# Token-mixing MLP products in pairs of tiles by Strassen's scheme: seven products of quarters in place of eight

## The chip, the cores and the metric

The kernel runs as one program on one core of one Trainium2 chip. The metric is the time of one execution on the device in microseconds (us). The kernel before takes 1084.5 us (the median of 3 runs, 1084.46 to 1085.56).

## The reference

A network of four layers on x of 2048 tokens (S) by 640 channels (D): a spectral filter A and a token-mixing MLP B, and the same two again with the same weights, each with a residual and a layer norm in front.

```python
def _A_ref(x, w_r, w_i):
    X = jnp.fft.rfft2(x, axes=(-2, -1)) * (w_r + 1j * w_i)
    return jnp.fft.irfft2(X, s=(S, D), axes=(-2, -1))

def _B_ref(x, w1, b1, w2, b2):          # F = 1728
    h = _layernorm(x, axis=-1)
    u = _gelu(jnp.einsum("bsd,sf->bdf", h, w1) + b1)
    y = jnp.einsum("bdf,fs->bds", u, w2) + b2
    return y.transpose(0, 2, 1)

x = A_x
x = x + _A_ref(_layernorm(x, axis=-1), A_w_r, A_w_i)
x = x + _B_ref(_layernorm(x, axis=-1), B_w1, B_b1, B_w2, B_b2)
x = x + _A_ref(_layernorm(x, axis=-1), A_w_r, A_w_i)
x = x + _B_ref(_layernorm(x, axis=-1), B_w1, B_b1, B_w2, B_b2)
```

## The kernel before, in words

The change is in the two MLP layers (`b(li)`: `first` is the first MLP layer, `last` the last layer of the network) and in the edges of the spectral parts `a1` and `a2` that prepare them. The float32 products of the MLP are made of three float16 ones: each operand is split into a high half (the value scaled by a power of two and rounded to float16) and a low half (what is left), and TensorE adds high·high, high·low and low·high in PSUM. For weights, ACT writes the high half `wh` from the float32 load `raw`, and DVE the low half `wl` = raw·s − wh; for the normed hidden state `hf` the halves are `hh` and `hl`, for the gelu's output `uh` and `ul`.

The first product of a layer has 14 tiles of 128 columns of F (`ft`); the last holds its 64 columns twice, which lets one of its three products be left out. Each tile sums over 16 row tiles `j` of the tokens, in two column halves of 320 (one PSUM bank each): 96 matmuls. The second product has 16 tiles of tokens that each sum over the 14 tiles of F. Tiles 0 and 1 of a layer begin with the products that need only `hh`, so that DVE has time for `hl`. After a tile ACT and DVE make the gelu: ACT `t` (affine) and `q` (square) from PSUM, a DVE step, ACT's tanh, a DVE step, then the split into `uh` and `ul`.

Weights are loaded as halves of 512 KB by SP's queue, three tiles ahead (`wload`), and split one tile ahead (`prep`, `wsplit`). In the first MLP layer the scale of each weight tile has to be found first: ACT squares the loads with a sum (`scan1`, tile `junk`), TensorE adds over the partitions, small steps on DVE and POOL make a power of two (`scale1`); the last layer uses the scales again. `scale_u` gives the scale of the gelu's output.

What runs on each engine is in program order, and in the MLP the order is that of the code (`self.pin = True` writes the instructions as they come; otherwise a planner may place them). Nearly all instructions go through one helper, line 46 (L46) of the profile of before, so groups are told apart by the names of tiles: `raw` weights as loaded, `ps` PSUM, `xt` the residual rows.

Of the kernel before, what the change touches and what calls it, by code (L numbers as in the profile page):

```python
# [18 lines left out]
NJ, NG, NFT = 16, 16, 14  # L19
EPS = 1e-5  # L20
# [3 lines left out]
HA = range(8)  # L24
# [4 lines left out]
US = 2.0 ** 14  # L29
# [3 lines left out]
EXPO = 0x7F800000  # L33

# [19 lines left out]
class Layers:  # L54
# [41 lines left out]
    def setup(self):  # L96
# [16 lines left out]
        self.qt = base.tile([128, NFT], F32, name="qt")  # L113
        self.su, self.iu = (base.tile([128, 1], F32, name=a) for a in ("su", "iu"))
# [41 lines left out]
    def total(self, sq):  # L156
# [6 lines left out]
        ps = self.big()[:, 0, :n]  # L163
        self.PE.matmul(ps, self.ones, b, start=True, stop=True)
        yield ps
# [17 lines left out]
    def scan1(self, m, cs=(0, 1)):  # L183
        if m < NFT + NJ:
            if 0 in cs:
                self.ssq = self.t(self.base, [128, 1, 2], F32, "sq", 2)
            for c in cs:
                self.scan(self.wraws[m][c], self.ssq[:, 0, c:c + 1])

    def scale1(self, m):  # L190

        V, (k, t, _) = self.V, self.wtile(m)
        c = slice(t, t + 1)
        q = self.t(self.base, [128, 1], F32, "q2", 2) if k else self.qt[:, c]
        for ps in self.total(self.ssq):
            yield
        V.tensor_scalar(q, ps, SMALL, WS ** -2, op0=ALU.max, op1=ALU.mult)
        i = self.pow2(q, self.st[k][:, c])
        V.tensor_scalar(self.ct[k][:, c], i, self.iu if k else 0.5 / ZS, None, op0=ALU.mult)
        yield  # L200
# [39 lines left out]
    def scale_u(self):  # L240

        V, b = self.V, self.base
        q, qc = (b.tile([128, 1], F32, name=a) for a in ("qm", "qc"))
        V.tensor_reduce(q, self.qt, op=ALU.max, axis=mybir.AxisListType.X)
        V.scalar_tensor_tensor(qc, q, 2.0 * S * D * (WS / US) ** 2, self.qb, op0=ALU.mult, op1=ALU.add)
        i = self.pow2(qc, self.su)
        V.tensor_scalar(self.iu, i, 0.125, None, op0=ALU.mult)
# [153 lines left out]
    def a1(self, first):  # L401
# [3 lines left out]
        ph = self.push("ha", side=self.sq)  # L405
        self.hh = {j: ph.tile([128, 2, 320], F16, name=f"hh{j}_{self.n}") for j in HA}
# [159 lines left out]
        quarter = lambda q: ((q // 2,), slice(q % 2 * 4, q % 2 * 4 + 4))  # L566
# [11 lines left out]
        for g in range(NG - 1):  # L578
# [18 lines left out]
            if 10 <= g < 14:  # L597
                self.wsplit(0, quarter(g - 10)[0], hi=False, part=quarter(g - 10)[1])
# [12 lines left out]
            if g == 3:  # L611
                self.wload(0)
                self.wopen(0)
# [4 lines left out]
            if first and g in (5, 6):  # L618
                self.scan1(0, (g - 5,))
            if first and g == 7:  # L620
                sc0 = self.scale1(0)
            if first and 7 <= g < 10:
                next(sc0)
            if 9 <= g < 13:
                self.wsplit(0, quarter(g - 9)[0], lo=False, part=quarter(g - 9)[1])
# [37 lines left out]
        self.pin = False  # L663
        self.pop("a1")
# [3 lines left out]
    def a2(self, li):  # L668
# [4 lines left out]
        self.wp[1] = self.push("wb", side=self.sp)  # L673
        ph = self.push("hf", side=self.sp)
        self.hf = [ph.tile([128, 2, 320], F32, name=f"hf{j}_{self.n}") for j in range(NJ)]
# [70 lines left out]
        for i in range(NJ + 3):  # L746
# [30 lines left out]
            if has[3]:  # L777
                r, b = rb.pop(i - 3)
                f = self.hf[i - 3]
                T.activation(f, xt.pop(i - 3)[:, :D].rearrange("p (a b) -> p a b", a=2), AF.Identity, scale=r, bias=b)  # L780
                if i - 3 in HA:
                    T.activation(self.hh[i - 3], f, AF.Copy)
            if i + 2 < NJ:
                xt[i + 2] = xload(i + 2)
            if i == 3:
                self.wload(1)
            if first:
                if i in (6, 7):
                    self.scan1(1, (i - 6,))
                if i == 8:  # L790
                    sc = self.scale1(1)
                if i in (8, 9, 10):
                    next(sc)
            if i == 3:
                self.wopen(1)
            if i in (12, 13):
                self.wsplit(1, (i - 12,), lo=False)
# [7 lines left out]
    def wtile(self, m):  # L805

        return (0, m, NJ) if m < NFT else (1, m - NFT, NFT)

    def wload(self, m):
        k, t, n = self.wtile(m)  # L810
        src = self.A["w2" if k else "w1"][t]
        raws = self.wraws[m] = []
        for c in (0, n // 2):
            raws.append(self.t(self.wr[max(m - 2, 0) % 3], [128, 8, 128], F32, "raw", 2)[:, :n // 2])
            self.nc.sync.dma_start(raws[-1], src[:, c:c + n // 2])

    def wopen(self, m):
        wh, wl = (self.t(self.wp[m % 2], [128, NJ, 128], F16, a, 1) for a in ("wh", "wl"))
        self.w[m] = wh, wl

    def wsplit(self, m, cs=(0, 1), hi=True, lo=True, part=slice(None)):

        V, T, (k, t, n) = self.V, self.T, self.wtile(m)
        sc = self.st[k][:, t:t + 1]
        (wh, wl), raws = self.w[m], self.wraws[m]
        for c in cs:
            raw, a = raws[c][:, part], slice(c * n // 2, c * n // 2 + n // 2)
            h, l = wh[:, a][:, part], wl[:, a][:, part]
            if m == NFT - 1:

                T.activation(h[:, :, :64], raw[:, :, :64], AF.Identity, scale=sc)
                T.activation(l[:, :, 64:], raw[:, :, 64:], AF.Identity, scale=sc)
                V.scalar_tensor_tensor(
                    h[:, :, 64:], raw[:, :, 64:], sc, l[:, :, 64:], op0=ALU.mult, op1=ALU.subtract
                )
                continue
            if hi:
                T.activation(h, raw, AF.Identity, scale=sc)
            if lo:
                V.scalar_tensor_tensor(l, raw, sc, h, op0=ALU.mult, op1=ALU.subtract)  # L840


    def b(self, li):
        nc, A = self.nc, self.A
        V, G, T = self.V, self.G, self.T
        mm = self.PE.matmul
        first, last = li == 1, li == 3
        ph = self.push("h", side=self.sq)
        for j in range(NJ):
            if j not in HA:  # L850
                self.hh[j] = ph.tile([128, 2, 320], F16, name=f"hh{j}_{self.n}")
                T.activation(self.hh[j], self.hf[j], AF.Copy)
        self.pin = True
        self.wsplit(1, hi=False)
        self.h = []
        for j in range(NJ):
            self.h.append((self.hh[j], ph.tile([128, 2, 320], F16, name=f"hl{j}_{self.n}")))
            V.tensor_tensor(self.h[j][1], self.hf[j], self.hh[j], op=ALU.subtract)
        self.pin = False
        self.pop("hf")  # L860
        self.wr[1:] = (self.push(a, side=self.sp) for a in ("wr", "wr2"))
        pu = self.push("u", side=self.sp)
        uh = [pu.tile([128, 2, 320], F16, name=f"uh{f}_{self.n}") for f in range(NFT)]
        ul = [pu.tile([128, 2, 320], F16, name=f"ul{f}_{self.n}") for f in range(NFT)]
        if first:
            pf = self.push("uf", side=self.sp)
            uf = [pf.tile([128, 2, 320], F32, name=f"uf{f}_{self.n}") for f in range(NFT)]
            sc = {m: self.scale1(m) for m in range(2, NFT + NJ)}
        p = self.push("b1", side=self.sq)
        for m in (2, 3, 4):  # L870
            self.wload(m)

        def ahead(m):

            if m + 3 < NFT + NJ:
                self.wload(m + 3)
            if m + 1 < NFT + NJ:
                self.wopen(m + 1)

        def prep(m):  # L880

            for c in range(2 if m + 1 < NFT + NJ else 0):
                self.wsplit(m + 1, (c,))
                yield

        def step(m):
            if first and m in sc:
                next(sc[m])

        def usplit(ft, t):  # L890
            if first:
                V.tensor_scalar(uh[ft], t, self.su, None, op0=ALU.mult)
            else:
                T.activation(uh[ft], t, AF.Identity, scale=self.su)
            c = slice(0 if ft < NFT - 1 else 64, 128)
            V.scalar_tensor_tensor(ul[ft][c], t[c], self.su[c], uh[ft][c], op0=ALU.mult, op1=ALU.subtract)
            if ft == NFT - 1:
                V.tensor_copy(ul[ft][:64], uh[ft][:64])

        def prod(ps, w, j, h, start=False, stop=False):  # L900
            for a in range(2):
                mm(ps[:, a, :320], w[:, j], h[:, a], start=start, stop=stop)

        def high(ft, ps, w):

            for j in range(NJ):
                yield j
                prod(ps, w[0], j, self.h[j][0], start=j == 0)
                prod(ps, w[1], j, self.h[j][0])

        def rest(ft, ps, w):
            for j in range(NJ):
                yield j
# [450 lines left out]
```

## Time and profile before

| | |
|---|---|
| median of 3 runs | 1084.5 us |
| the profiled execution | 1084.86 us; its span 1083.1 us, granted TensorE clock 0.974 |
| TensorE busy | 1030.8 us (95%), 8515 matmuls |
| DVE, ACT, POOL busy | 643.6 (59%), 553.9 (51%), 289.4 us (27%) |
| DMA | 141.48 MB, mean 131 GB/s |

The span in 40 slices of 27 us; digits are tenths of the slice that the engine was busy:

```profile
PE   4889798999999999999997998999999999999998
DVE  7979879954335856566746995995343334223221
ACT  5857768675445555555432775864433344222220
POOL 6938877200000002211221886840000000000000
```

The first spectral part is slices 1 to 8, the first MLP 9 to 21, the second spectral part 22 to 26, and the last MLP 27 to 40. In the first MLP ACT is busier than in the last by the squares for the scales.

### The profile page before, as it was taken

To read this page: it belongs to the slowest core of one execution; us is meant where nothing else is said; L and a number is where in the kernel's file an instruction comes from. 1 tells how busy PE (TensorE), PEld (TensorE's weight loads), DVE (VectorE), ACT (ScalarE), POOL (GpSimd) and SP (SyncE) were. 2 spreads that over 40 slices of the span, in tenths; PEclk is the share of its full clock that TensorE was granted. 3 is DMA by queue.
4 is the path that set the end of the run, shared out by engine and by line. 5 is a ranking of instruction groups with operands and counts; after the bars stand their busy time and mean duration, and the time that the engine had idled before them with its cause. 6 is when DMAs were issued, how large, how long until landed. Compare 5 with 4: busy or idle time off the path is not lost.

```text
span 1083.1 us, 21299 instructions
## 1 busy us (share of the span) xinstructions
PE 1030.8 (95%) x8515; PEld 777.2 (72%) x8515; DVE 643.6 (59%) x1311; ACT 553.9 (51%) x860; POOL 289.4 (27%) x491
## 2 busy tenths in 40 slices
PE   4889798999999999999997998999999999999998
PEld 3768698777777767777776878877777776666665
DVE  7979879954335856566746995995343334223221
ACT  5857768675445555555432775864433344222220
POOL 6938877200000002211221886840000000000000
PEclk8599999999999999999998998999999999999999
DMA  7766255523222264444224633644222233433411
GB/s 234 255 192 193 80 195 184 185 89 104 82 79 68 69 240 134 138 126 130 84 76 129 207 97 130 212 146 156 83 91 81 81 106 113 161 118 133 158 51 37
DMA packets 55738, 141.48 MB, mean 131 GB/s; under 512 B 6460, under 2 KB 12248, under 8 KB 55384
## 3 DMA queue, kind: packets, MB, share of 16 engines
q1 hardware_dynamic: 54200, 131.97, 37.5%
q0 software_dynamic: 1440, 8.15, 2.4%
q8 instruction: 67, 1.10, 0.4%
q14 instruction: 31, 0.25, 0.1%
HBM read 117.03 MB, written 23.07 MB: 129 GB/s over the span
## 4 chain that ended last, share of the span: by engine, by line
PE 76%; DVE 16%; POOL 2%; issue 2%; ACT 1%; DMA 1%; SPq 0%; DVEq 0%; ACTq 0%; POOLq 0%
PE ps L46 76%; DVE xt L46 5%; DVE st L46 2%; DVE el L46 2%; DVE f L46 2%; DVE s1l L46 1%; DVE hl L46 1%; DVE ta L46 1%; DVE xl L46 1%; DMA xt<-x 1%; POOL eo L46 0%; POOL ta L46 0%; DMA rest<-s1l 0%; DVE tb L46 0%; DVE mv L46 0%
## 5 line engine op out<-in xcount | busy, mean ns | idle before, releaser
L46 PEld LDWEIGHTS <-wh 128*128 128x128 f16 x3520 | 340.0, 98 | 138.3 <-issue 1.8
L46 PE MATMUL ps<-uh,wl 128*128 128x320 f16 (+1 forms) x896 | 268.4, 300 | 0.0
L46 PE MATMUL ps<-ul,wh 128*128 128x320 f16 x896 | 267.3, 299 | 0.0
L46 PE MATMUL ps<-uh,wh 128*128 128x320 f16 x832 | 248.9, 299 | 0.0
L46 PEld LDWEIGHTS <-wl 128*128 128x128 f16 x1728 | 168.7, 98 | 76.6 <-issue 8.7
L46 DVE SCALAR_TENSOR_TENSOR wl<-raw,s,wh 128x896 f16<-128x896 f32 (+2 forms) x120 | 139.2, 1173 | 112.9 <-ACT wh L46 112.6
L46 PE MATMUL ps<-hh,wh 128*128 128x320 f16 x896 | 194.8, 299 | 1.4 <-ACT hh L46 1.4
L46 ACT ACTIVATE wh<-raw,s 128x896 f16<-128x896 f32 (+2 forms) x124 | 126.6, 1044 | 131.0 <-PE ps L46 130.3
L46 PE MATMUL ps<-hl,wh 128*128 128x320 f16 x896 | 184.8, 299 | 0.0
L46 PE MATMUL ps<-hh,wl 128*128 128x320 f16 x832 | 181.1, 299 | 0.0
L46 POOL TENSOR_TENSOR r<-v,mh 128x1 f32<-128x1 f32 x64 | 35.8, 559 | 340.8 <-DVE nm L46 325.3
L46 DVE SCALAR_TENSOR_TENSOR xt<-ps,c,xt 128x640 f32<-128x640 f32 (+1 forms) x33 | 28.4, 863 | 139.6 <-PE ps L46 135.9
L46 ACT ACTIVATE junk<-raw 128x896 bf16<-128x896 f32 (+1 forms) x60 | 59.6, 993 | 48.5 <-DMA raw<-w 48.3
L46 ACT ACTIVATE xt<-xt,b2s 128x640 f32<-128x640 f32 x32 | 26.3, 821 | 91.1 <-DMA xt<-x 90.9
L46 DVE TENSOR_TENSOR f<-eo 128x256 f32<-128x256 f32 (+1 forms) x128 | 40.1, 366 | 41.8 <-POOL eo L46 41.2
L46 PE MATMUL ps<-tDi,yh 128*128 128x322 f32 x256 | 61.1, 326 | 2.6 <-ACT yh L46 1.7
L46 DVE BATCH_NORM_STATS2 st<-xt 128x6 f32<-128x320 f32 x128 | 56.2, 481 | 5.1 <-DMA xt<-x 4.9
L46 POOL TENSOR_TENSOR eo<-z 128x320 f32<-128x320 f32 x63 | 54.2, 881 | 17.0 <-ACT z L46 15.1
L46 PE MATMUL ps<-ph,tS 128*128 128x321 f16 (+2 forms) x288 | 57.9, 286 | 0.0
L46 PE MATMUL ps<-tM,f 128*128 128x128 f32 x160 | 38.3, 409 | 20.4 <-DMA xt<-x 11.9
L46 ACT ACTIVATE z<-xt,nb,r 128x640 f32<-128x640 f32 x31 | 28.5, 919 | 54.1 <-POOL z L46 43.6
L46 PEld LDWEIGHTS ps<-tM,f 128*128 128x128 f32 x160 | 32.3, 290 | 26.2 <-DVE f L46 25.7
(142 smaller groups left out, 1678.9 us busy)
## 6 DMA issues: line engine op xcount, KB each, us to landing
raw<-w SPq DMA_DIRECT2D x56, 512.0 KB
raw<-w SPq DMA_DIRECT2D x64, 448.0 KB
xt<-x SPq DMA_DIRECT2D x80, 320.0 KB
w<-w SPq DMA_DIRECT2D x48, 321.0 KB
x<-xt SPq DMA_DIRECT2D x48, 320.0 KB
out<-xt SPq DMA_DIRECT2D x15, 320.0 KB
tIM<-tIM POOLq DMA_DIRECT2D x8, 512.0 KB, 4.7
tDi<-tDi POOLq DMA_DIRECT2D x2, 1932.0 KB, 9.9
```

What stands on the lines that cost most here:

```text
L46: i = f(*a, **k)
```

## The change

Strassen's scheme in Winograd's form multiplies a 2x2 block matrix of weights A by a 2x2 block matrix B with seven products: A11·B11, S1·T1, S2·T2, S3·T3, A12·B21, S4·B22, A22·T4, with S1 = A21 + A22, S2 = S1 − A11, S3 = A11 − A21, S4 = A12 − S2 and T1 = B12 − B11, T2 = B22 − T1, T3 = B22 − B12, T4 = B21 − T2 (signs as the code has them), and adds up the four results from them. Here two tiles of output (`t` and `t + 7` of F, or `d` and `d + 8` of the tokens) are the rows of A, the halves of the sum its columns, and the two column halves of 320 the columns of B. Three products take it: the first product of both MLP layers (pairs 1 to 6; tiles 0 and 7 stay as they were) and the second product of the last layer (8 pairs). The second product of the first layer keeps plain tiles.

- The sums S of the raw weights are made on POOL (`G`), in float32, 128x1024 each (128x896 in the second product), in the place of a load where that is possible; then each of the seven operands is split on ACT (high) and DVE (low) as before. The names are now `wo` for the two halves of an operand and `s` for S1.
- T1 to T3 of the hidden state are made on DVE, T4 on POOL, each 128x2560, once a layer; their halves are `hhT` and `hlT` (T4 takes the place of the quarter of `hh` and `hl` that only tile 0 and 7 needed). In the last layer the same is done on `u` for the second product, tile by tile.
- The results of the seven products are added from PSUM: on ACT and DVE (`evict1`, `finish`: tiles `m`, `u`, `f`) for the first product, on DVE and POOL (`evict2`) for the second.
- F is padded from 1728 to 2·896 columns, 32 in each half, so the tile with the doubled 64 columns is gone.
- Memory for loads and operands is kept in lists of free places (`slots`, `place`); an operand is split when a place is free, at most 6 products ahead (`advance(n + 6)`). In the first layer the scale is found for a pair (four squares), as is the scale of the gelu's output, `su`, by pairs; `again` brings `u` to one common scale ahead of the second product.

The core of the diff (the plumbing of pools and the first tiles are cut):

```diff
+        PQ = ("A11", "B11"), ("S1", "T1"), ("S2", "T2"), ("S3", "T3"), ("A12", "B21"), ("S4", "B22"), ("A22", "T4")
+        ops = [(0, t, *q) for t in range(1, NP) for q in PQ]
...
+                if a == "S1":
+                    s1[k, t] = self.t(pA, [128, 8, 128], F32, "s1", 1)[:, :7 if k else 8]
+                    G.tensor_tensor(s1[k, t], q[1, 0], q[1, 1], op=ADD)
+                if a == "S3":
+                    G.tensor_tensor(q[1, 0], q[0, 0], q[1, 0], op=SUB)
+                if a == "S2":
+                    G.tensor_tensor(q[0, 0], s1[k, t], q[0, 0], op=SUB)
+                if a == "S4":
+                    G.tensor_tensor(q[0, 1], q[0, 1], q[0, 0], op=SUB)
...
+        def wsplit(k, t, a):
...
+            if a == "A11":
+                sums(k, t, "S1")
+            self.split((k, t, a), scale(k, t), src=s1[k, t] if a == "S1" else self.raw[key[src[a]]][0])
+            if a == "A11":
+                sums(k, t, "S3", "S2")
+            if a == "A12":
+                sums(k, t, "S4")
...
+        def finish(t, X, Y, m):
...
+            add(0, X[:, 0], m["m1"])
+            add(1, Y[:, 0], m["u4"])
+            half(q0, f[:, :2], f[:, :2], coef(t, 0))
+            add(3, X[:, 1], m["u3"])
+            if t < NP - 1:
+                add(2, Y[:, 1], m["u3"])
+                gelu0(q0, f[:, :2])
+                half(q1, f[:, 2:4], f[:, 2:4], coef(t, 1))
+                gelu1(q0, f[:, :2])
+                gelu0(q1, f[:, 2:4])
+                yield
+                gelu1(q1, f[:, 2:4])
...
+        for n in range(nprod):
+            k, t, a, b = ops[n]
...
+            product(k, t, a, b, range((7 if k else 8) - late))
...
+            if not late or n == N1 + 3:
+                while pending:
+                    evict(pending.pop())
+            for f in sched.get(n, ()):
+                f()
+            advance(n + 6)
```

The second product's `evict2` adds `ps`·c to the residual quarters `x` on DVE (scalar_tensor_tensor, 128x320), seven a pair, with four 128x320 sums on POOL.

Three places show how the rows stand now. First DVE at the start of the last layer. Before, the low halves of tile 7's weights were followed by the sixteen of the hidden state (`hl`) and then by the first gelu step (`q`), with a low split of weights after it:

```order
L46 TENSOR_TENSOR hl_1492_10340<-hf_1275_9386,hh_1492_10306 128x640
L46 TENSOR_TENSOR hl_1492_10342<-hf_1275_9387,hh_1492_10308 128x640
L46 SCALAR_TENSOR_TENSOR q_10560<-q_10560,t_10559 128x640
L46 SCALAR_TENSOR_TENSOR wl_10569<-raw_10385,s_72,wh_10568 128x1024
L46 SCALAR_TENSOR_TENSOR t_10559<-q_10560,t_10559 128x640
```

Now, from the same point, with the first six operands of the first pair (`wo_1558` to `wo_1560` are A11, S1 and S2):

```order
L55 TENSOR_TENSOR hl_10266<-hf_1321_9357,hh_7808 128x2x320 x8
L55 TENSOR_TENSOR hf_1321_9357<-hf_1321_9357 128x2560
L55 TENSOR_TENSOR hl_10267<-hf_1321_9358,hh_10265 128x2x320 x8
L55 TENSOR_TENSOR hf_1321_9357<-hf_1321_9358,hf_1321_9357 128x2560
L55 TENSOR_TENSOR hf_1321_9358<-hf_1321_9358,hf_1321_9357 128x2560
L55 SCALAR_TENSOR_TENSOR wo_1558_10516<-raw_1549_10280,s_72,wo_1558_10516 128x1024
L55 TENSOR_TENSOR hlT_10269<-hf_1321_9357,hhT_10268 128x2560
L55 SCALAR_TENSOR_TENSOR wo_1559_10522<-s_1557_10514,s_72,wo_1559_10522 128x1024
L55 TENSOR_TENSOR hlT_10269<-hf_1321_9358,hhT_10268 128x2560
L55 SCALAR_TENSOR_TENSOR wo_1560_10527<-raw_1549_10280,s_72,wo_1560_10527 128x1024
```

Three differences of the hidden state (T1, T3, T2) stand ahead of the first weight split, and each of the next two splits stands behind a low half of a T.

Second, DVE in the middle of the last layer's first product. Before, one tile had:

```order
L46 SCALAR_TENSOR_TENSOR q_10607<-q_10607,t_10606 128x640
L46 SCALAR_TENSOR_TENSOR wl_10621<-raw_10389,s_72,wh_10620 128x1024
L46 SCALAR_TENSOR_TENSOR t_10606<-q_10607,t_10606 128x640
L46 SCALAR_TENSOR_TENSOR wl_10621<-raw_10391,s_72,wh_10620 128x1024
L46 SCALAR_TENSOR_TENSOR ul_1495_10369<-t_10606,su,uh_1495_10355 128x640
```

Now part of a pair (`wo_1583` is A12, `wo_1587` S4, `wo_1593` A22, `wo_1596` A11 of the next pair):

```order
L55 SCALAR_TENSOR_TENSOR wo_1583_10782<-raw_1565_10569,s_72,wo_1583_10782 128x1024
L55 SCALAR_TENSOR_TENSOR wo_1587_10814<-raw_1565_10569,s_72,wo_1587_10814 128x1024
L55 TENSOR_TENSOR f_10817<-ps_10300,m_1567_10597 128x320
L55 TENSOR_TENSOR f_10817<-ps_10301,u_1579_10723 128x320
L55 TENSOR_TENSOR f_10817<-ps_10300,u_1578_10722 128x320
L55 TENSOR_TENSOR f_10817<-ps_10301,u_1578_10722 128x320
L55 SCALAR_TENSOR_TENSOR q_10818<-q_10818,f_10817 128x640
L55 SCALAR_TENSOR_TENSOR f_10817<-q_10818,f_10817 128x640
L55 SCALAR_TENSOR_TENSOR q_10819<-q_10819,f_10817 128x640
L55 SCALAR_TENSOR_TENSOR wo_1593_10860<-raw_1552_10296,s_72,wo_1593_10860 128x1024
L55 SCALAR_TENSOR_TENSOR f_10817<-q_10819,f_10817 128x640
L55 SCALAR_TENSOR_TENSOR wo_1596_10893<-raw_1582_10756,s_72,wo_1596_10893 128x1024
```

The splits of A12 and S4 stand next to each other and read the same place (`raw_1565`), which POOL fills with S4 between them; the gelu of the pair before follows.

Third, POOL at the end of the second spectral part. Before, its last rows were small ones of the layer norm, and there was nothing in the last MLP:

```order
L46 TENSOR_TENSOR xt_1276_9391<-xt_1276_9391,ec_10256 128x321
L46 TENSOR_TENSOR r_10272<-v_10265,mh 128x1
L46 TENSOR_TENSOR nb_10274<-nm_10267,r_10272 128x1
L46 TENSOR_TENSOR r_10283<-v_10279,mh 128x1
```

Now the sums begin there (S1, S3, S2, then T4, S4, and the next pair's):

```order
L55 TENSOR_TENSOR s_1557_10514<-raw_1547_10276,raw_1548_10278 128x1024
L55 TENSOR_TENSOR raw_1547_10276<-raw_1549_10280,raw_1547_10276 128x1024
L55 TENSOR_TENSOR raw_1549_10280<-s_1557_10514,raw_1549_10280 128x1024
L55 TENSOR_TENSOR hf_1321_9358<-hf_1321_9358 128x2560
L55 TENSOR_TENSOR raw_1550_10282<-raw_1550_10282,raw_1549_10280 128x1024
L55 TENSOR_TENSOR s_1569_10602<-raw_1551_10294,raw_1552_10296 128x1024
L55 TENSOR_TENSOR raw_1551_10294<-raw_1564_10567,raw_1551_10294 128x1024
```

The rows go on by fours for each pair, in the order S1, S3, S2, S4, through both products of the layer.

More of the change, by code (lines that the diff above doesn't have):

```diff
@@ L33, with pair @@
 EXPO = 0x7F800000
+KT = [[(0, t, c) for c in range(2)] for t in (0, NP)]
+def pair(k, t):
+    return {(i, c): (k, t + i * (NQ if k else NP), c) for i in range(2) for c in range(2)}
 class Pin:
@@ L802, in a2 @@
         self.pop("Y")
[L805 to L840, printed above, removed]
+    def slots(self, kind, pool, n, temp=False):
+        for _ in range(n):
+            self.n += 1
+            self.free[kind].append((pool, f"{kind}{self.n}", temp))
@@ L847, in b @@
         first, last = li == 1, li == 3
+        ADD, SUB, MUL = ALU.add, ALU.subtract, ALU.mult
         ph = self.push("h", side=self.sq)
[L849 to L852, printed above, removed]
-        self.pin = True
[L854 to L858, printed above, removed]
@@ L859, in b @@
-        self.pin = False
[L860 to L913, printed above, removed]
-                prod(ps, w[0], j, self.h[j][1], stop=j == NJ - 1)
@@ new lines, in b, with advance @@
+        done = set()
+        nxt = [0]
+        def advance(n):
+            while nxt[0] < min(n, len(ops)) and self.free["wo"]:
+                k, t, a, c = ops[nxt[0]]
+                if a is None:
+                    if not ((k, t) in ready and any(not q[2] for q in self.free["wo"])):
+                        return
+                    self.split((k, t, c), self.st[1][:, t:t + 1], keep=True)
+                    self.release((k, t, c))
+                else:
+                    if first and (k, t) not in ready or not all(q in self.raw for q in pair(k, t).values()) and a == "A11":
+                        return
+                    wsplit(k, t, a)
+                nxt[0] += 1
+            if nxt[0] < nprod and ops[nxt[0]][2] == "A11":
+                k, t = ops[nxt[0]][:2]
+                if all(q in self.raw for q in pair(k, t).values()) and (not first or (k, t) in ready):
+                    sums(k, t, "S1")
@@ new lines, in b @@
+        keys = lambda k, t: list(pair(k, t).values())
+        if first:
+            for i in range(4):
+                self.qscan(keys(0, 1), i)
+        tsplit("T1", (0,))
+        for j in range(8, NJ):
+            hsplit(j)
+        scq = {}
+        if first:
+            scq[1] = self.qscale(0, 1, at=lambda: bank["Y"])
+            next(scq[1])
+        V.tensor_tensor(fT["T3"], f1[:, 1], f0[:, 1], op=SUB)
+        V.tensor_tensor(fT["T2"], f1[:, 1], fT["T1"], op=SUB)
+        rest(0, range(8))
@@ new lines, in b @@
+        if first:
+            next(scq[1])
+        rest(0, range(8, NJ))
+        rest(1, range(NJ))
+        for i in range(2):
+            for key in KT[i]:
+                self.unsplit(key)
+        if first:
+            next(scq[1])
+            ready.add((0, 1))
+        advance(1)
+        tsplit("T1", (1,))
+        if first:
+            self.scale_u(0)
+            self.scale_u(1)
+        advance(2)
+        tsplit("T2")
+        advance(3)
+        tsplit("T3")
+        G.tensor_tensor(fT["T4"], f1[:, 0], fT["T2"], op=SUB)
```

624 lines of the change are left out of this document (453 added, 171 removed).

## The prediction, made before the change was run

> **What bounds the kernel now.** I read the page first, then the chain of waits, then stretches of the timeline. In the page:
>
> ```profile
> span 1083.1 us, 21299 instructions
> PE 1030.8 (95%) x8515; PEld 777.2 (72%) x8515; DVE 643.6 (59%) x1311; ACT 553.9 (51%) x860; POOL 289.4 (27%) x491
> PE 76%; DVE 16%; POOL 2%; issue 2%; ACT 1%; DMA 1%; SPq 0%; DVEq 0%; ACTq 0%; POOLq 0%
> ```
>
> The profiled execution took 1084.86 us, 1.76 us more than its span and 0.36 us over the median of the three runs (1084.5 us). I work against its own time. TensorE ends most of the chain. The chain in order of time shows where:
>
> ```profile
> 216.88 355.79 PE ps L46 x2707
> ...
> 723.37 355.66 PE ps L46 x2568
> 1079.05 0.55 DVE xt L46
> ```
>
> The two MLP layers are two unbroken TensorE stretches. Busy time by stretch (PE, PEld, DVE, ACT, POOL) inside the last layer's first product, and the groups of TensorE in 60 us of the first layer's:
>
> ```profile
> 730.00:900.00 170.00, 170.00 (x1253) 122.47 (x1252) 72.88 (x77) 74.92 (x89) 0.00 (x0) 1.00 0.30 97
> ```
>
> ```profile
> L46 PE MATMUL ps<-hl,wh 128*128 128x320 f16 x148 | 32.2, 299 | 0.0
> L46 PE MATMUL ps<-hh,wh 128*128 128x320 f16 x148 | 32.2, 299 | 0.0
> L46 PE MATMUL ps<-hh,wl 128*128 128x320 f16 x147 | 32.0, 299 | 0.0
> ```
>
> 443 matmuls in 60 us is 0.1354 us each (the 299 ns overlap). POOL does nothing there and DVE is 43% busy, so weights are always ready.
>
> **What is removed.** The code gives the counts. A product of two plain tiles has 2·16·2·3 = 192 matmuls, seven quarter products 7·8·3 = 168. Each first product goes from 1,312 to 192 + 6·168 = 1,200. The last layer's second product goes from 1,312 to 8·7·7·3 = 1,176. The first layer's second product grows from 1,312 to 1,344, as the padded tile loses the old shortcut for its half. In time: −15.2, −15.2, −18.4 and +4.3 us, together −328 matmuls, **−44.4 us**, if TensorE never waits.
>
> **What is added**, per pair: four sums of raw weights on POOL, seven splits (ACT high, DVE low) in place of four, sums of PSUM quarters on DVE, and, once a layer, differences of the hidden state. All of it stands in a fixed order on each engine. Prices are start to start:
>
> ```profile
> 721.50 2.48 DVE L46 SCALAR_TENSOR_TENSOR wl<-raw,s,wh 128x1024 f16<-128x1024 f32 x2
> 723.88 11.85 DVE L46 TENSOR_TENSOR hl<-hf,hh 128x640 f16<-128x640 f32 x16
> 739.47 0.82 DVE L46 SCALAR_TENSOR_TENSOR q<-q,t 128x640 f32<-128x640 f32 x1 [3.73 <-ACT q L46]
> 740.50 1.28 DVE L46 SCALAR_TENSOR_TENSOR wl<-raw,s,wh 128x1024 f16<-128x1024 f32 x1 [0.21 <-ACT wh L46]
> 741.70 0.82 DVE L46 SCALAR_TENSOR_TENSOR t<-q,t 128x640 f32<-128x640 f32 x1
> ```
>
> ```profile
> 737.77 0.89 ACT L46 ACTIVATE t<-ps,b1s,c 128x640 f32<-128x640 f32 x1 [13.83 <-PE ps L46]
> 738.56 0.88 ACT L46 ACTIVATE q<-ps,b1s,c 128x640 f32<-128x640 f32 x1
> 739.33 1.14 ACT L46 ACTIVATE wh<-raw,s 128x1024 f16<-128x1024 f32 x1
> 740.37 0.73 ACT L46 ACTIVATE q<-q 128x640 f32<-128x640 f32 x1
> 740.99 1.14 ACT L46 ACTIVATE wh<-raw,s 128x1024 f16<-128x1024 f32 x1
> ```
>
> DVE: a low split of 1024 takes 1.20 us; 640 elements 0.74 (11.85/16). ACT: a split 1.04, the gelu's first two operations 0.78 each, tanh 0.62. For shapes not in the trace I also use this pair of 320-wide sums from PSUM, and these POOL rows:
>
> ```profile
> 179.39 0.89 DVE L46 TENSOR_TENSOR xt<-xt,ps 128x320 f32<-128x320 f32 x2
> ```
>
> ```profile
> 422.05 1.68 POOL L46 TENSOR_TENSOR eo<-z 128x320 f32<-128x320 f32 x2 [1.00 <-ACT z L46]
> ```
>
> ```profile
> 173.65 0.89 POOL L46 TENSOR_TENSOR xt<-xt,ec 128x321 f32<-128x321 f32 x1
> 174.48 1.30 POOL L46 TENSOR_TENSOR yl<-Y,yh 128x512 fp32r<-128x512 f32 x1
> ```
>
> A sum of 320 costs DVE 0.40. By the slope from 320 to 640, 1920 elements cost 2.1 and 2560 cost 2.8 (bound: 4·0.74 = 3.0). POOL needs 0.84 for 320 and 1.30 for 512; 1024 is then 1.30 + 512·2.4 ns = 2.5 us (two of 512 bound it at 2.6), 896 is 2.2, 2560 about 6.2.
>
> **Two engines that stop each other.** DVE at the same moment:
>
> ```profile
> 173.40 2.74 DVE L46 TENSOR_TENSOR xt<-xt,ec 128x320 f32<-128x320 f32 x1
> ```
>
> This sum of two SBUF tiles costs 0.40 to 0.48 us alone. Here it ended at 176.14, 0.36 us after both POOL instructions (175.78). The pair with a PSUM operand at 179.39 kept its 0.89 us. So a DVE operation with two SBUF inputs waits while POOL runs a sum; all low splits and gelu steps are of that kind. "SBUF — State Buffer" of the Trainium skill, section "SBUF: two separate sides", says the shared port pair is an exclusive lock held for a whole instruction. The trace agrees (those 2.74 us). By that rule alone each POOL sum stands in DVE's way in full, which is the rival of the locked port below.
>
> **Start of a layer (last one).** T is 721.50, where DVE starts on the low halves of tile 7.
>
> ```profile
> 723.37 0.43 PE L46 MATMUL ps<-hh,wh 128*128 128x320 f16 x2 [0.69 <-ACT hh L46]
> ```
>
> At 723.37 TensorE has 132 plain matmuls left, so it is free for the first pair at T+19.7. DVE's row before the first low split of a quarter is 2·1.2 + 16·0.74 + 3·2.8, and the split ends at T+23.8: a wait of 4.1. The next three products need 2.8 + 1.2 = 4.0 of DVE each against 24·0.1354 = 3.25 of TensorE: 2.3 more. The seventh waits for the low half of T4 behind another gelu step and split: 2.3. That is 8.7 us with POOL free of charge. With the lock, two sums of 2.5 before the first split, and one of 2.5 plus the 6.2 of T4 before the second and third, bring it to 21. Before, no such wait was there (0.69). I take 14.
>
> **Start (first layer).** There the scale must come first: four squares on ACT, a column sum on TensorE that stands between the halves of tile 0, then small steps. Loads land about 2.9 us apart:
>
> ```profile
> 207.18 1.06 ACT L46 ACTIVATE junk<-raw 128x1024 bf16<-128x1024 f32 x1 [2.22 <-DMA raw<-w]
> ...
> 209.99 1.06 ACT L46 ACTIVATE junk<-raw 128x1024 bf16<-128x1024 f32 x1 [1.66 <-DMA raw<-w]
> ```
>
> One load goes first, so the pair's fourth lands near 219 and its square ends at 222, 19.8 after the low splits began at 202.5; TensorE has run dry 6.1 earlier. The small steps behind the differences add 2.2, fourteen more before the second product 3.3, ACT's four further squares ahead of the seventh 5.6, the rest 2.9: 20 us, with the lock 28. I take 23.
>
> **A steady pair, last layer.** TensorE needs 168·0.1354 = 22.75. DVE's row: seven low splits 8.4, four gelu steps 3.0, seven PSUM sums 2.8, four differences 1.6, two u splits 2.5: 18.3. In its order it also stands still: 2.3 for gelu's ACT steps (the second half's two come before the first tanh), 1.7 for the 1,920-wide u split on ACT, and 3.7 at S4: POOL may form it only after the split of A12 (2.5), then ACT (1.04), then DVE, with nothing between. 26.0 us: 3.2 over. Splits six products ahead don't help, since the period itself is too long. With the lock the next pair's S1 pushes S4 by 1.3 and S2 stops the differences for 2.5: 7.0 over. I take 5, between, since POOL may find a gap. The second pair lives on the start, so four pairs: **20** (13 to 28). In the first layer DVE has no differences and smaller u splits, but fourteen scale steps at 0.19 (2.7), and ACT four squares: 24.2 to 30, so 1.4 to 7.2 over. I take 4: **16** (6 to 29).
>
> Last layer's second product: DVE needs 7·1.05 + 7·0.40 + 2.9 = 13 and POOL 4·2.2 + 4·0.84 = 12.2 of 19.9 us. It is covered even if the two take turns (25 only if nothing overlaps); 1 (0 to 5). DMA: four loads of 0.5 MB take 12 of 22.75 us, hidden. The tail after the last matmul keeps its kind.
>
> **The clock.** TensorE waited at the end of the first layer, and for ACT's `Y` before 653.12; the granted share of the stretches around (third column from the right) was:
>
> ```profile
> 653.12 0.40 PE L46 MATMUL ps<-tI,xh 64*128 64x128 f16 x4 [2.06 <-ACT Y L46]
> ```
>
> ```profile
> 573.00:590.00 17.00, 10.94 (x117) 9.20 (x115) 11.41 (x24) 4.89 (x9) 2.16 (x3) 0.80 0.45 146
> ...
> 620.00:664.00 44.00, 38.44 (x577) 32.34 (x572) 32.18 (x50) 28.84 (x56) 32.41 (x51) 0.88 0.36 105
> ```
>
> Half speed for some 7 us costs up to 3.5 where TensorE is the bound. The start waits may bring it on, but there DVE is the bound: 0. "TensorE: Matmul & The Clock Gate" (Trainium skill, "Part 1: The HAM clock gate") puts the window at about 3.4 us of idleness. By it the waits of a steady pair would never slow the clock, while the row at 653.12 has less idleness (2.06) in a stretch that fell to 0.88: the measurement is the stricter.
>
> **Sum**: 1084.9 − 44.4 + 23 + 16 + 14 + 20 + 1 = **1114 us**. All low ends: −44.4 + 20 + 6 + 8.7 + 13 + 0 gives 1088; all high: 28 + 29 + 21 + 28 + 5 gives 1151.
>
> **Rivals.**
> - *The look-ahead covers* (other side, faster): the splits run six products ahead. If DVE's stops in a pair overlap other work so that a period stays under 22.75, only starts remain: −44.4 + 8.7 + 12 = **1061** (1048 to 1078). For it: ACT and DVE were under half busy. Against: DVE's row has no spare order. It decides if the period is below 22.75.
> - *Even*: half of the stops above: 1084.9 − 44.4 + 43 = **1084**.
> - *Locked port*: all four POOL sums land on DVE, 2.5 each for those not yet counted: periods near 33.5, ten over in eight pairs, plus 49 for the starts: 1084.9 − 44.4 + 49 + 80 = **1170**. Against: POOL sums also run while DVE waits for ACT or reads PSUM.
>
> **How the numbers follow.** 0.58 for the forecast (1088 to 1151), 0.26 for the cover, 0.06 for even, 0.10 for the locked port. Runs of this kernel differ by 0.1%; 0.2%, 2 us, is about what a measurement can tell. The even case is split: 0.05 same, the rest to either side, so 0.27 faster, 0.68 slower. The range 1060 to 1150 leaves out half of the fastest case and most of the locked one.
>
> **What would show it.** Right: TensorE idle in first products, ended by DVE's low splits; DVE idle on ACT's high split of S4 with POOL behind it; low splits longer than 1.3 us beside POOL sums; the last second product dense. Wrong: first products with TensorE at 100% as in the row of 730 to 900; pair periods of 22.8 us.

## The result: 1246.0 us, 15% slower

The changed kernel takes 1246.0 us (median of 4 runs, 1244.8 to 1248.8) against 1085.0 (median of 4 runs of the kernel before, taken with it); the ratio is 1.148 (95% interval 1.146 to 1.151). The forecast was 1114 (1060 to 1150). From the page of the changed kernel:

```profile
span 1243.1 us, 21215 instructions
PE 1024.4 (82%) x8181; PEld 765.5 (62%) x8181; DVE 904.2 (73%) x1535; ACT 661.4 (53%) x963; POOL 549.8 (44%) x605
...
PE   4899888548888799999989989863777786889988
...
PEclk8699899878989999999989989987888888889999
```

334 matmuls fewer stand in the trace, but TensorE is only 6.4 us less busy (1030.8 before), as its granted clock (lower row) falls in three of the four products. The busy time in the first layer's first product and the last layer's two products (stretch and its length; PE, PEld, DVE, ACT, POOL; then granted clock, DMA share, GB/s):

```profile
197.00:440.50 243.50, 184.24 (x1215) 124.37 (x1215) 181.94 (x276) 137.83 (x176) 75.02 (x32) 0.88 0.21 69
...
781.00:1038.00 257.00, 180.97 (x1200) 122.92 (x1199) 186.14 (x188) 112.22 (x117) 86.55 (x35) 0.85 0.20 65
1038.00:1239.00 201.00, 172.39 (x1177) 119.35 (x1175) 124.56 (x124) 75.13 (x89) 104.76 (x61) 0.92 0.32 108
```

At 0.1354 us a matmul the 1200 of the last layer's first product would take 162.5 us; of its 257.0 us, 18.5 go to slower matmuls and 76.0 to waits. What ended these waits (total, times, longest):

```profile
PE ps L55 <- DVE u L55: 61.9, 6, 18.7
PE ps L55 <- DVE wo L55: 5.1, 3, 2.6
```

So it is DVE's sums out of PSUM (`u`), not its splits of weights (`wo`), that TensorE waits for. Lengths of the four products from first to last matmul, in us (the names are those of the experiments below):

| kernel | first layer, 1st | first layer, 2nd | last layer, 1st | last layer, 2nd | time |
|---|---|---|---|---|---|
| before | 181.8 | 196.2 | 180.4 | 185.0 | 1085.0 |
| changed | 243.2 | 196.0 | 257.4 | 200.8 | 1246.0 |
| s4_early | 230.4 | 196.6 | 245.0 | 199.8 | 1222.2 |
| evict_first | 240.0 | 194.5 | 229.7 | 202.9 | 1214.2 |
| s4_and_evict | 237.3 | 194.3 | 225.9 | 203.6 | 1208.6 |
| no_pool_sums | 201.5 | 195.1 | 214.3 | 172.2 | 1133.1 |
| no_pool_evict | 201.0 | 194.4 | 178.5 | 176.4 | 1096.9 |
| sums_on_dve | 240.6 | 196.7 | 246.8 | 179.7 | 1210.8 |
| dve_all_three | 225.0 | 195.1 | 210.7 | 181.4 | 1158.7 |
| fill_the_wait | 242.9 | 195.6 | 251.0 | 200.2 | 1238.9 |
| second_only | 190.3 | 195.8 | 186.0 | 171.8 | 1094.2 |
| second_only_2 | 186.0 | 203.6 | 182.8 | 172.9 | 1093.0 |
| second_only_3 | 181.5 | 203.7 | 178.4 | 173.0 | 1082.7 |
| second_only_4 | 181.1 | 199.0 | 178.4 | 172.9 | 1078.2 |

A steady pair of the last layer's first product is 34.0 us long where TensorE needs 22.75. Here u2 and u3 are the results of S2 and S3, which DVE adds up from one PSUM tile; S4's product writes that tile next, so it waits for both. The timeline of PE, DVE, ACT and POOL (start, length, idle before and what ended it):

```profile
961.60 0.42 PE L55 MATMUL ps<-hh,wo 128*128 128x320 f16 x1 [8.76 <-DVE u L55]
...
962.08 0.74 PE L55 MATMUL ps<-hh,wo 128*128 128x320 f16 x2
```

```profile
951.40 3.96 DVE L55 TENSOR_TENSOR f<-f 128x320 f32<-128x320 f32 x4
...
957.33 2.22 DVE L55 SCALAR_TENSOR_TENSOR u<-f,su,u 128x1920 f16<-128x1920 f32 x1 [1.50 <-ACT u L55]
...
961.06 0.88 DVE L55 TENSOR_TENSOR u<-ps,u 128x320 f32<-128x320 f32 x2
...
968.44 1.28 DVE L55 SCALAR_TENSOR_TENSOR wo<-raw,s,wo 128x1024 f16<-128x1024 f32 x1 [4.11 <-ACT wo L55]
973.43 2.18 DVE L55 SCALAR_TENSOR_TENSOR wo<-raw,s,wo 128x1024 f16<-128x1024 f32 x1 [3.70 <-ACT wo L55]
```

```profile
967.26 1.15 ACT L55 ACTIVATE wo<-raw,s 128x1024 f16<-128x1024 f32 x1 [6.85 <-PE ps L55]
972.25 1.15 ACT L55 ACTIVATE wo<-raw,s 128x1024 f16<-128x1024 f32 x1 [3.83 <-POOL raw L55]
```

```profile
969.86 2.35 POOL L55 TENSOR_TENSOR raw<-raw,raw 128x1024 f32<-128x1024 f32 x1 [15.77 <-issue]
```

This is a closed loop: each step waits for the one before it, and the last one starts the first again. TensorE starts S4's product at 961.60, when DVE has taken u3 out of PSUM. When that product ends, its operand place is free and ACT splits the next pair's A12 into it (967.26); DVE makes the low half (968.44), POOL forms S4 in the place of A12's raw quarter (969.86), ACT and DVE split it (972.25, 973.43), then follow in DVE's row the gelu, the differences `f`, the split of `u` and at last the next u3, 34 us after the one before.

### The profile page after: what moved, and what is told of

The parts are those of the page before. It is cut to its first block, busy times and chain, and to the rows that moved or that the text cites. A ratio compares the mean times of both kernels' runs of the same rounds, so it can differ in the third digit from the quotient of the medians.

```text
span 1243.1 us, 21215 instructions
## 1 busy us (share of the span) xinstructions
PE 1024.4 (82%) x8181; PEld 765.5 (62%) x8181; DVE 904.2 (73%) x1535; ACT 661.4 (53%) x963; POOL 549.8 (44%) x605
## 5 line engine op out<-in xcount | busy, mean ns | idle before, releaser
L55 PEld LDWEIGHTS <-wo 128*128 128x128 f16 x4920 | 495.5, 101 | 382.9 <-issue 133.4
L55 PE MATMUL ps<-u,wo 128*128 128x320 f16 x2520 | 358.2, 305 | 29.3 <-DVE u L55 18.2
L55 DVE SCALAR_TENSOR_TENSOR wo<-raw,s,wo 128x896 f16<-128x896 f32 (+2 forms) x164 | 227.8, 1400 | 120.1 <-ACT wo L55 120.0
L55 ACT ACTIVATE wo<-raw,s 128x896 f16<-128x896 f32 (+2 forms) x164 | 172.4, 1068 | 239.7 <-POOL raw L55 142.5
L55 PE MATMUL ps<-hh,wo 128*128 128x320 f16 x1024 | 212.4, 316 | 81.9 <-DVE u L55 72.5
L55 POOL TENSOR_TENSOR raw<-raw,raw 128x1024 f32<-128x1024 f32 (+1 forms) x40 | 104.5, 2611 | 210.5 <-issue 197.2
L55 PE MATMUL ps<-hhT,wo 128*128 128x320 f16 x576 | 132.8, 321 | 28.8 <-DVE qt L55 16.3
L55 PE MATMUL ps<-hl,wo 128*128 128x320 f16 x512 | 139.7, 312 | 0.6 <-DVE hl L55 0.6
L55 POOL TENSOR_TENSOR raw<-s,raw 128x1024 f32<-128x1024 f32 (+1 forms) x20 | 57.9, 2893 | 125.9 <-DVE wo L55 101.7
L55 PE MATMUL ps<-hlT,wo 128*128 128x320 f16 x288 | 92.6, 322 | 4.8 <-DVE hlT L55 4.8
L55 DVE TENSOR_TENSOR f<-eo 128x256 f32<-128x256 f32 (+1 forms) x128 | 40.1, 366 | 44.4 <-POOL eo L55 43.7
```

The costliest lines, as they stand in the source:

```text
L55: i = f(*a, **k)
```

## The experiments

The expectations set three explanations against each other. In the loop theory a pair lasts as long as the loop above. In the lock theory POOL's sums stop DVE wherever they stand. In the DVE-row theory, the prediction's, a pair lasts as long as DVE's own work and stops, in whatever order.

**S4 out of the loop (s4_early).** POOL writes S4 over S2's place.

```diff
-  G.tensor_tensor(q[0, 1], q[0, 1], q[0, 0], op=SUB)   # behind the split of A12
+  G.tensor_tensor(q[0, 0], q[0, 1], q[0, 0], op=SUB)   # behind the split of S2
...
-            if a == "A12":
+            if a == "S2":
                 sums(k, t, "S4")
```

> S4 is written over S2's place instead of A12's, so POOL forms it right after the split of S2 and the splits of A12 and S4 no longer wait for POOL between them. Loop theory (TensorE's S4 product frees the operand place for the next A12; its splits, POOL's S4, the S4 split, the gelu and the evictions u2, u3 follow one another, and u3 lets TensorE start the next S4 product): the POOL sum (2.4 us) and the ACT split behind it (1.2) leave the loop, 3.5 us for each of some 10 pairs of the first products and 2.5 for each of 7 of the second, about 1190 us. Lock theory (POOL's sums stop DVE wherever they stand): the sums are as many and as long, so within 10 us of 1246.

1222.2 us (ratio to before 1.126, 1.123 to 1.130): 24 us less, of the 56 expected by the loop theory, nearly all in the two first products. In the second product the pairs kept their 24.2 us, so another chain holds them; the lock theory's "within 10 us of 1246" fell too.

**Evictions (the sums out of PSUM) ahead of the split of u (evict_first).**

```diff
             while not u:
                 yield
+            yield
             usplit(0, f)
...
                 gelu1(q1, f[:, 2:4])
+                yield
+                yield
                 yield
                 usplit(t, f)
```

> The differences and halves of u (usplit) are put two steps later, behind the evictions u2, u3 and u4 of the next pair; nothing else moves. Loop theory: in the last layer's first product 8 us of DVE's row between the gelu and u3 leave the loop, and with them the wait of 8.8 us and the half clock behind it: pairs of 34 us fall to about 25 there; in the first layer only the wait of 0.7 us goes, since there the column sum's reader (qt) holds TensorE; the second product stays: about 1200 us. DVE-row theory (as predicted: a pair lasts as long as DVE's row with its stops, in whatever order): no change, within 5 us of 1246.

1214.2 us (1.118, 1.116 to 1.121). The last layer's first product fell by 27.7 us, the first layer's by 3, the second product not: as the loop had it, against the prediction's view that DVE's row counts in any order. But pairs came to 29.5 us, not 25.

**Both (s4_and_evict).**

> Both edits. Loop theory: about 1150 us (the gains add up but for the pairs that reach DVE's own row, about 24 us). DVE-row theory: as s4_early alone. Lock theory: above 1200.

1208.6 us (1.114, 1.112 to 1.116), above the 1150 of the loop theory; only the lock theory's "above 1200" held. With both out of the way pairs still took 29.2 us, and DVE was busy for 25.2 of them:

```profile
928.00:957.00 29.00, 24.65 (x168) 17.14 (x168) 25.22 (x25) 14.99 (x16) 9.61 (x5) 0.94 0.20 68
```

Two rows of that pair show why: S1's low split, 1.2 us alone, and four differences, 1.8 alone (in the rows of dve_all_three below). POOL's sums began at 927.61 (2.34 us), 933.10 (2.53) and 935.59 (2.60), beside them:

```profile
927.78 3.25 DVE L55 SCALAR_TENSOR_TENSOR wo<-s,s,wo 128x1024 f16<-128x1024 f32 x1
...
932.95 6.12 DVE L55 TENSOR_TENSOR f<-f 128x320 f32<-128x320 f32 x4
```

**No POOL sums (no_pool_sums).**

```diff
-  G.tensor_tensor(s1[k, t], q[1, 0], q[1, 1], op=ADD)   # and S2, S3, S4, T4
```

> All sums on POOL in the two MLP layers are left out (the operands are split from plain quarters and T4 from plain hidden state; the four additions of results to xt stay), all else stands. Loop theory: as s4_early (the sum leaves the loop), about 1190 us, and less by what the lock costs where DVE is in the loop. Lock theory: DVE's stretched splits (5.5 to 8.2 us for 2.4 to 2.8) go, 3 us a pair and some 20 us at the starts: about 1120 us, 60 to 70 us under s4_early.

1133.1 us (1.045, 1.043 to 1.046): 113 us less than the changed kernel, 13 above the lock theory's 1120 and far below the loop theory's 1190. In the second product TensorE waits once, 10.0 us at its start. DVE's busy time falls from 904.2 to 816.8 us with the same 1535 instructions, so its operations had been stretched by 87 us in all. The 113 us are more than the lock, though: with the sums go the waits of ACT and DVE for their results, and no run keeps the sums while nothing waits for them.

**No POOL sums, and the evictions first (no_pool_evict).**

> POOL's sums left out as in no_pool_sums, and usplit behind the evictions. If order and lock are the two causes, pairs of the last layer's first product fall from 29 us (no_pool_sums) to DVE's bare row, 18.3 + 3.7 = 22 us, which TensorE's 22.75 covers: no waits in steady pairs, about 1095 us. If a third cause stands there: pairs stay above 25, about 1120.

1096.9 us (1.011, 1.009 to 1.013). The two causes add up: POOL's sums cost 113 us with the old order and 117 with the new, the order 32 with the sums and 36 without. A steady pair of the last layer now runs at TensorE's pace and full clock:

```profile
853.00:876.00 23.00, 23.00 (x171) 16.47 (x170) 18.76 (x24) 14.72 (x17) 0.00 (x0) 1.00 0.29 91
```

The waits left to TensorE are 28.3 us in the first layer's first product (11.7 for column sums, 5.8 for their reader `qt`), 10.5 in the last layer's, and 10.3 at the start of its second product.

**The sums on DVE (sums_on_dve).**

```diff
-  G.tensor_tensor(s1[k, t], q[1, 0], q[1, 1], op=ADD)   # all S, T4, and the sums into xt
+  V.tensor_tensor(s1[k, t], q[1, 0], q[1, 1], op=ADD)
```

> All sums that POOL made in the two MLP layers (S1 to S4, T4, and the four additions to xt of each pair of the second product) are made by DVE at the same places of the program. Lock theory (a POOL sum of 2.35 us holds up every DVE operation on two SBUF tiles for its whole length, while DVE itself needs about 1.1 for it): faster, the second product dense at 20 us a pair (24.2 now, 28 us in all), T4's 5.6 us and the stretched splits at the starts gone (15), pairs of the first products 1 to 3 us shorter (20): about 1180 us. Loop theory alone (S4 sum in the loop): the sum is 1.2 shorter there, the other sums lengthen DVE's row by 1.1 each: 1235 to 1250.

1210.8 us (1.116, 1.114 to 1.118). The second product is 21 us shorter, with DVE busier and POOL empty; its pairs take 21.0 us for 24.2. Two things changed there at once: DVE is no longer stopped, and the sums in the chain are themselves shorter (1.1 us for 2.1 at 128x896). How the 21 us divide between them is not shown. The changed kernel, then this one:

```profile
1090.00:1190.00 100.00, 88.94 (x599) 61.20 (x599) 68.38 (x60) 38.52 (x44) 60.61 (x35) 0.92 0.39 127
```

```profile
1090.00:1190.00 100.00, 95.60 (x701) 68.25 (x699) 81.54 (x107) 42.12 (x47) 0.00 (x0) 1.00 0.40 130
```

In the first products, where the old order keeps the loop, little was won (13 us): the expected 1180 was missed there.

**All three edits (dve_all_three).**

> Sums on DVE, S4 over S2's place, and usplit behind the evictions. If what is left after the two edits of order (pairs of 29.2 us) is DVE's row stretched by the lock, a pair of the last layer's first product is 18.3 + 4 sums of 1.13 + 3.7 of waits for ACT = 26.5 us, the first layer's about 26 and the second product dense: about 1130 us. If the lock is not what is left: 1190 or more.

1158.7 us (1.067, 1.066 to 1.069). Pairs of the last layer's first product: 27.7 us for 26.5 expected; DVE's own sums take 1.23 us where POOL's took 2.35:

```profile
904.92 1.23 DVE L55 TENSOR_TENSOR raw<-s,raw 128x1024 f32<-128x1024 f32 x1
906.06 0.48 DVE L55 TENSOR_TENSOR u<-ps,m 128x320 f32<-128x320 f32 x1
906.46 1.27 DVE L55 SCALAR_TENSOR_TENSOR wo<-s,s,wo 128x1024 f16<-128x1024 f32 x1
...
910.91 1.81 DVE L55 TENSOR_TENSOR f<-f 128x320 f32<-128x320 f32 x4
```

With the sums in its row DVE is busy 23.7 us of a pair (905 to 933), more than TensorE's 22.75, so the scheme in the first products stays above TensorE's pace even without POOL and with the shorter loop.

**The half clock (fill_the_wait).**

```diff
+            if last and k == 0 and a == "A12" and t > 1:
+                for i in range(120):
+                    mm(bank["X"][:, 0, 336:464], self.w[k, t, a][0][:, 0, i % 8], h0[:, 0, i % 8, :128], start=True, stop=True)
```

> The changed kernel, with 120 matmuls of 128 columns whose results nobody reads put behind each A12 product of pairs 2 to 6 of the last layer's first product (some 7 of the 8.8 us in which TensorE waits). If the half clock after the wait lies on the loop (S4's product 5.6 us instead of 3.25), these pairs fall from 34.0 to about 31.7 us, 12 us in all: 1234. If the clock is off the loop: 1246 or a little more.

1238.9 us (ratio 1.142, 1.139 to 1.144): 7 us faster with 600 matmuls more, some 60% of what was expected. In two stretches of about a pair the clock was full in one and 0.95 in the other:

```profile
927.00:960.00 33.00, 29.68 (x288) 23.16 (x288) 23.13 (x26) 16.12 (x17) 10.36 (x4) 1.00 0.21 65
960.00:994.00 34.00, 31.39 (x289) 23.89 (x289) 22.47 (x27) 15.21 (x16) 10.35 (x4) 0.95 0.19 59
```

From S4's product to the next, the pair that begins at 928.79 at full clock took 31.8 us, the 31.7 expected; the one that begins at 960.54, with matmuls 0.27 us apart behind a wait of 2.07, took 33.4. So the clock is on the loop: slow matmuls behind a wait lengthen the round.

**A kernel faster than both (second_only, then _2, _3 and _4).** The scheme in the last layer's second product alone, where DVE has room; first products with plain quarter operands.

```diff
-        ops = [(0, t, *q) for t in range(1, NP) for q in PQ]
+        ops = [(0, t, f"A{i + 1}{c + 1}", c) for t in range(1, NP) for i in range(2) for c in range(2)]
...
```

> Strassen's scheme in the last layer's second product alone, with S4 over S2's place and all sums on DVE; the first products of both layers take four plain quarter operands for each pair of tiles (1,344 matmuls, for the tile with doubled columns is gone) and have no differences of the hidden state. If order and lock are the whole cause, all four products are dense: the second product's 1,176 matmuls of 0.1354 us take 160 us (185 before), the first products 182 each (181.8 and 180.4 before), with some 5 us more at the start of the first layer, where a pair's scale waits for four loads: 1085 - 25 + 2 + 5, about 1067 us, faster than both kernels. If a pair scheme costs something else even here: 1080 or more.

1094.2 us (1.009, 1.007 to 1.010), not 1067: pairs took 21.0 us, the second product began with a wait for ACT, which stood behind a load of x, and in both layers TensorE waited 2.5 us for ACT's `hh`. The row of the first wait:

```profile
928.03 24.65 PE L55 MATMUL ps<-u,wo 128*128 128x320 f16 x168 [3.46 <-ACT m L55]
```

> second_only with three waits taken away: A11's result leaves PSUM right behind its own product (ACT's copy waited for S1's product too, which writes the other bank of the same tile, and the loop copy, splits, sums, u2, u3, S4's product took 21.0 us for 19.9 of matmuls); the first pair's rows of x are loaded six products earlier and get their bias behind that copy (ACT stood 3.7 us for that load in front of TensorE); and the last tile of F holds its 64 columns twice again in the first products (64 matmuls less in all). Loop theory: pairs of 19.9 us (8 us in all), 5 us at the start of the second product, 8.7 for the matmuls: 1072 us, about 1% faster than the kernel before. If the wait of 0.9 us a pair isn't from that copy: 1080.

1093.0 us (1.007, 1.005 to 1.008), not 1072. Pairs fell only to 20.7; some 7 us won in the first products (the doubled columns) were lost in the first layer's second product, where the last rows of u came too late.

> second_only_2 with three edits of order: the high halves of the second eight rows of the hidden state may again be placed among the last work of the spectral part (TensorE waited 2.5 us for them at the start of both layers and ran at half clock behind it: 4 us each); in the first layer the gelu of tile 6 is emitted as soon as its sum is complete (the second product waited 5.7 us for the last gelu, 7 with the half clock); and the last layer has four more places for loads (ACT waited 3.3 us for one). 1093 - 8 - 7 - 3, about 1075 us, faster than the kernel before. If the half clock costs nothing where it stands: 1084 or more.

1082.7 us (0.998, 0.997 to 0.999), not 1075. The starts gave their share; the wait of 5.7 us for the last gelu stayed, and DVE's row shows what stood ahead of it:

```profile
373.71 0.16 DVE L55 TENSOR_SCALAR q<-ps 128x1 f32<-128x1 f32 x1 [7.44 <-PE ps L55]
```

> second_only_3 with one edit: in the first layer the scales of the second product's first two tiles are read from PSUM one product earlier, before the next product writes the same PSUM tile. DVE waited 7.4 us for that product with the last gelu steps behind it, and TensorE then 5.7 us for the last rows of u, 28 matmuls at half clock behind it. Expected 1083 - 7.5, about 1075 us (0.990 of the kernel before); if a PSUM tile's reader does not wait for a write to other columns of it, no change.

1078.2 us (0.994, 0.993 to 0.996), 4.5 us of the 7.5 expected: the wait of 5.66 us fell to 2.68, so in this kernel that read of one PSUM column had stood behind a product into other columns of the same tile. This kernel beats the one before by 0.6%; the last second product gives 12 us (172.9 for 185.0), of which the rest of the program takes half back.

## Why the prediction was wrong

- *Matmuls removed*: the count held, but TensorE's busy time fell by 6.4 us and not by 44.4; most of the rest went to the clock. The step "DVE is the bound: 0" for the half clock failed: behind most waits of 2.5 us and more, matmuls ran 0.27 us apart for some 3 to 6 us (three took 0.80 at 962.08; in sums_on_dve the same came behind waits of 2.0 us, as at 296.53), and by the rows above some 18.5 us in the last first product alone went so. How many of these are on the path, fill_the_wait shows for five pairs alone (7 us).
- *A steady pair* was forecast at 27.75 us in the last layer and 26.8 in the first, as DVE's row with its stops for ACT and S4; it took 34.0 and 29.5. The failed step was to let DVE run free of TensorE ("the period itself is too long"): the order of the evictions and the operand places tie both into a loop. Putting the evictions first took 32 to 36 us off the kernel. With both edits of order s4_and_evict gave 29.2, near the 29.8 of the prediction's locked row. In the first layer the loop closed elsewhere: TensorE waited 4.07 us a pair for `qt`, the reader of the column sum, behind the gelu in DVE's row.
- *The lock* was seen and named, but halved by choice ("POOL may find a gap"). POOL's sums cost 113 to 117 us with all that waits for them; the part that is DVE's stretched work is 87 us of busy time, and how much of that lay on the path is not shown. The rival of the locked port (1170) came nearest and missed the loop and the clock. That its period of 33.5 us is close to the measured 34.0 is luck: DVE was busy for only 21.9 of them. The Trainium skill's "SBUF — State Buffer" (section "SBUF: two separate sides") calls it an exclusive lock for a whole instruction; the trace agrees: beside T4's sum, which ended at 825.71, a low half that takes 2.8 us alone took 8.22 and ended 2.7 us later.

```profile
819.12 6.59 POOL L55 TENSOR_TENSOR hf<-hf 128x2560 f32<-128x2560 f32 x1
```

```profile
820.17 8.22 DVE L55 TENSOR_TENSOR hlT<-hf,hhT 128x2560 f16<-128x2560 f32 x1
```

- *The second product* ("covered even if the two take turns", 1 us) was the smallest term of the sum and off by some 33 us: the product became 15.8 us longer where 17 less were forecast. The prediction's own sums, 13 us for DVE and 12.2 for POOL, make 25 if they take turns, against 19.9 for TensorE; it set the 25 aside, and pairs took 24.2. The turns stood in a chain from A11's result over the splits to u3, with two splits of 1.1 us each stretched to 5.85 together; TensorE waited 18.2 us for u3. Another 10.2 us, in none of the forecast's terms, were one wait at the start for ACT's copy of A11's result, as ACT itself stood 3.8 us for a load of x; this wait is as long without POOL's sums (10.0). Behind the waits the clock fell to 0.92.

```profile
1130.79 5.85 DVE L55 SCALAR_TENSOR_TENSOR wo<-raw,s,wo 128x896 f16<-128x896 f32 x2 [1.10 <-ACT wo L55]
```

- *The starts*: waits up to the first S4 product were 34 us in the first layer and 32 in the last, for 23 and 14 forecast (the terms named for the last layer's locked start make 22.4, where the prediction has 21). no_pool_sums and evict_first both shortened them (the last layer's longest wait, 18.7 us, fell to 13.2 and 12.8). In the first layer the next pair's column sum held TensorE for 10.4 us, as its squares on ACT stood behind the split of S4; this was not in the sum.
- *Plain tiles and the padding*: the first layer's second product was to grow by 4.3 us for 32 more matmuls and stayed the same (196.2 and 196.0). The kernel before pays there for the last tile of F, whose 64 columns become matmuls of 64 rows. Where one of these meets one of 128 rows, the next start comes 0.23 to 0.24 us later and not 0.136: the weight load of the first one below (last row) begins 0.22 us behind the start of the matmul ahead, while a load of 128 rows there begins together with a matmul (both at 904.51). The trace of before has 64 such starts in the first layer's second product and 63 in the last layer's, some 6.5 us each. The padding removes them, so the last second product was worth some 25 us by matmuls alone, 18.4 for the count and 6.5 for these; even second_only_4 kept only 12.

```profile
904.51 0.30 PE L46 MATMUL ps<-uh,wl 128*128 128x320 f16 x1
904.65 0.30 PE L46 MATMUL ps<-ul,wh 128*128 128x320 f16 x1
904.88 0.31 PE L46 MATMUL ps<-uh,wl 64*128 64x320 f16 x1
905.12 0.31 PE L46 MATMUL ps<-ul,wh 128*128 128x320 f16 x1
```

```profile
904.51 0.10 PEld L46 LDWEIGHTS <-wh 128*128 128x128 f16 x1
904.87 0.09 PEld L46 LDWEIGHTS <-wl 64*128 64x128 f16 x1 [0.26 <-issue]
```

- *Right*: the direction, and the signs named for POOL: DVE idle on ACT's split of S4 with POOL behind it, and low splits longer than 1.3 us beside POOL's sums. The sign that DVE's low splits end TensorE's idle time held only at the starts (5.1 of 76.0 us in the last layer's first product, against 61.9 for `u`), and the last second product was not dense.
- A slip that decides nothing: half of the stops, for the even case, is 37 us and not 43.

What stays open: how the 113 us of POOL's sums divide between the lock and the waits for their results; and how much of the clock's loss is on the path outside the five pairs that were filled.

## What to carry to other kernels

Saving TensorE work pays only where the other engines have room in their order, not only in their sum of busy time: follow one round from a product's start to the next over evictions, freed places and splits before counting matmuls. A sum of two SBUF tiles given to POOL because it is idle could stop DVE for up to 2.35 us, in which DVE could have done the sum itself in 1.2; give POOL such work only where DVE reads PSUM or rests. Here it paid to put what returns PSUM to TensorE ahead of the splits of `u` in DVE's row.

## What the hardware showed beyond that

The lock stops even a tiny DVE operation with two tensor inputs: in the first layer a 128x1 step of the scale took 4.51 us beside T4's sum and ended with it (243.17 and 243.15). A step with one tensor input just ahead, beside the same sum, took 0.15, and the same two-input step with POOL at rest 0.16.

```profile
237.56 5.59 POOL L55 TENSOR_TENSOR hf<-hf 128x2560 f32<-128x2560 f32 x1
```

```profile
238.40 0.15 DVE L55 TENSOR_SCALAR iu<-qi 128x1 f32<-128x1 f32 x1
...
238.66 4.51 DVE L55 SCALAR_TENSOR_TENSOR qc<-qm,qb 128x1 f32<-128x1 f32 x1
...
335.15 0.16 DVE L55 SCALAR_TENSOR_TENSOR qc<-qm,qb 128x1 f32<-128x1 f32 x1
```
